# Attention and bilinear FFN in float32 on one core: softmax with keys on partitions and no maximum, head products issued in turn, FFN in blocks of 384 and 512 tokens

## The chip, the core and the metric

The kernel runs on one core of a Trainium2 chip. The metric is the device time of one execution in microseconds (us), median over runs. The engines named below are PE (TensorE, matmuls; PEld is its weight load), DVE (VectorE), ACT (ScalarE), POOL (GpSimd) and SP (SyncE), which here issues all DMAs. Each engine takes its instructions in program order.

## The reference, cut to what matters

```python
# q, k, v: (8, 12, 448, 64) float32; g_q, g_k: (64,); w_a, w_b: (768, 1536), w_out: (1536, 768), in float64
def rmsnorm(x, g):
    return x / np.sqrt(np.mean(x * x, axis=-1, keepdims=True) + 1e-06) * g
scores = np.matmul(rmsnorm(q, g_q), rmsnorm(k, g_k).transpose(0, 1, 3, 2)) / np.sqrt(64)
scores = scores - np.max(scores, axis=-1, keepdims=True)
attn = np.exp(scores)
attn = attn / (np.sum(attn, axis=-1, keepdims=True) + 1e-09)
x = np.matmul(attn, v).transpose(0, 2, 1, 3).reshape(8 * 448, 12 * 64)
out = ((x @ w_a) * (x @ w_b)) @ w_out
```

## The kernel before, in words

Everything is float32. There are 8 batches of 448 tokens and 12 heads of 64 features. Attention goes by pairs of heads (48 pairs, 6 in each batch), and inside a pair by quarters of 112 queries, so the main loop has 192 steps `i`, four to a pair. A pair's q and k are normalised (`normalize`: squares and a power on POOL, sums and products on DVE), transposed on PE and copied out of PSUM with the gains (`transpose_qk`).

A step `i` makes the scores of 112 queries against 448 keys for both heads (`scores`, L180: queries on partitions), their maximum (DVE, L183), the exponential with its sum (ACT, L184), and the division (POOL, L188). `transpose_e` turns the result round on PE (L198) and copies it out (L200 and L202), one step later. `values` multiplies it with v (L212) two steps later; all four products of the first head stand there ahead of those of the second.

The FFN of batch b - 1 fills PE during the attention of batch b. `ffn` is a generator that yields after each piece: 24 groups of six matmuls (tile `pf`, L229) and 16 half groups of six matmuls (tile `po`, L242). `some(share)` runs as many pieces as are due. It starts at step 2 of a batch and is drained at step 1 of the next, so that two steps of each batch have no pieces. Three PSUM banks (`ps_mm`) hold the FFN's results.

The weights come as float64 in 72 units of 128 x 384 numbers. `round_weights` makes float32 of one unit: six DVE instructions (L116 to L122), one on ACT (L123), two on POOL (L124, L125). Tiles `mag` and `low` have one buffer, so a unit's DVE work starts when POOL has read the `mag` of the unit before. Two units stand in each of the first 36 steps. The order of all instructions is the order in which the code is written (`manual_schedule`).

## Time and profile before

| | |
|---|---|
| median of 3 runs | 2462.69 us (2460.68 to 2463.14) |
| span of the profiled execution | 2462.0 us, which is 0.7 us under that median |
| PE busy | 2135.5 us, 87% of the span |
| POOL, DVE, ACT busy | 927.3, 863.8 and 507.3 us |
| granted TensorE clock, mean | 0.92 |

The profile covers one execution, from its first to its last instruction. Busy time is the time in which an engine executes; a float32 matmul appears in it as two records (two passes over the same columns), while a transpose is one. A granted clock of 1.00 is 2.4 GHz and 0.50 is 1.2 GHz.

### The profile page before, as it was taken

What the parts mean: (1) busy time and instruction counts of PE and PEld (TensorE: products, weight loads), DVE (VectorE), ACT (ScalarE), POOL (GpSimd) and SP (SyncE); (2) the same over time, 40 slices, a digit from 0 to 9 for tenths busy, and PEclk for the clock granted to TensorE, in tenths of its full rate; (3) what the DMA queues carried; (4) which work ended last, traced back from release to release, by engine and by line L of the source; (5) the groups of instructions that cost most, each with busy time, mean ns of one, the idle gap of its engine ahead of it and who ended that gap; (6) DMA issues with size and microseconds to landing.
All of it is one profiled execution on the core that took longest, in us unless ns stands there. A gap on an engine that the chain in (4) does not pass through costs nothing.

```text
span 2462.0 us, 24929 instructions
## 1 busy us (share of the span) xinstructions
PE 2135.5 (87%) x9600; PEld 1223.7 (50%) x9600; DVE 863.8 (35%) x1809; ACT 507.3 (21%) x1257; POOL 927.3 (38%) x679
## 2 busy tenths in 40 slices
PE   3444448889999998999899998999899989999999
PEld 1332224445555554555555564555455545555555
DVE  5666665663232232322322323223222323222000
ACT  1221122222222222222222122222222212222100
POOL 5656555553333343433423333333333343332000
PEclk9566558889999998999899998999999999999999
DMA  3222222110100010000100010001100010000000
GB/s 91 65 73 62 63 77 62 53 48 24 33 17 18 7 37 25 12 16 23 42 12 12 17 35 17 23 4 32 33 12 12 24 33 23 12 10 15 3 0 23
DMA packets 53558, 73.95 MB, mean 30 GB/s; under 512 B 4801, under 2 KB 44225, under 8 KB 53441
## 3 DMA queue, kind: packets, MB, share of 16 engines
q1 hardware_dynamic: 53440, 72.37, 10.3%
q8 instruction: 76, 1.25, 0.2%
q14 instruction: 42, 0.34, 0.0%
HBM read 61.34 MB, written 11.01 MB: 29 GB/s over the span
## 4 chain that ended last, share of the span: by engine, by line
PE 73%; DVE 14%; POOL 7%; issue 3%; ACT 3%; DMA 0%; SPq 0%; POOLq 0%; ACTq 0%; DVEq 0%
PE pf L229 32%; PE po L242 21%; PE o L212 8%; PE sc L180 6%; PE pt L198 5%; POOL ms L146 3%; ACT E L184 2%; DVE mag L118 2%; POOL sq L142 2%; POOL low L124 1%; POOL E L188 1%; DVE ms L143 1%; PE pt L161 1%; DVE qkn L149 1%; DVE nmax L183 1%
## 5 line engine op out<-in xcount | busy, mean ns | idle before, releaser
L188 POOL TENSOR_SCALAR E<-E,sums 112x448 f32<-112x448 f32 x384 | 538.0, 1413 | 1118.0 <-DVE sums L186 892.2
L242 PE MATMUL po<-w_out_sb,hT 128*112 128x384 f32 x1536 | 519.7, 490 | 0.0
L229 PE MATMUL pf<-xT,w_b_sb 128*128 128x448 f32 x1152 | 470.7, 560 | 13.1 <-ACT hT L232 13.1
L229 PE MATMUL pf<-xT,w_a_sb 128*128 128x448 f32 x1152 | 459.1, 548 | 6.6 <-ACT qkT L166 5.8
L198 PE MATMUL pt<-ident,E 112*112 112x112 f32 x1536 | 210.5, 280 | 272.8 <-ACT ET L202 173.4
L184 ACT ACTIVATE E<-sc,nmax 112x448 f32<-112x448 f32 x384 | 240.1, 630 | 853.3 <-DVE nmax L183 853.3
L242 PEld LDWEIGHTS po<-w_out_sb,hT 128*112 128x112 f32 x1536 | 262.6, 177 | 233.1 <-issue 42.3
L183 DVE TENSOR_REDUCE nmax<-sc 112x1 f32<-112x448 f32 x384 | 221.3, 618 | 405.8 <-PE sc L180 405.8
L198 PEld LDWEIGHTS pt<-ident,E 112*112 112x112 f32 x1536 | 171.0, 144 | 361.0 <-issue 326.0
L229 PEld LDWEIGHTS pf<-xT,w_b_sb 128*128 128x128 f32 x1152 | 219.4, 196 | 230.0 <-issue 216.5
L229 PEld LDWEIGHTS pf<-xT,w_a_sb 128*128 128x128 f32 x1152 | 213.9, 192 | 228.2 <-issue 219.2
L212 PEld LDWEIGHTS o<-ET,v 112*64 112x64 f32 x3072 | 261.7, 150 | 94.9 <-issue 90.8
L212 PE MATMUL o<-ET,v 112*64 112x112 f32 x3072 | 306.6, 287 | 0.0
L180 PE MATMUL sc<-qkT 64*112 64x448 f32 x768 | 215.2, 637 | 17.8 <-ACT E L184 17.1
L234 DVE TENSOR_TENSOR hT<-hT,pf 128x448 f32<-128x448 f32 x96 | 59.5, 619 | 303.1 <-PE pf L229 303.1
L146 POOL TENSOR_TENSOR ms<-ms,expo 112x16 f32<-112x16 f32 x48 | 140.7, 2931 | 48.4 <-DVE ms L145 48.4
L143 DVE TENSOR_REDUCE ms<-sq 112x8 f32<-112x512 f32 x96 | 65.8, 686 | 244.3 <-POOL sq L142 244.3
L200 DVE COPY ET<-pt 112x448 f32<-112x448 f32 x192 | 118.6, 618 | 64.9 <-PE pt L198 62.6
L202 ACT COPY ET<-pt 112x448 f32<-112x448 f32 x192 | 101.9, 531 | 154.1 <-PE pt L198 154.1
L124 POOL TENSOR_TENSOR low<-low,mag 128x384 f32<-128x384 f32 x72 | 71.7, 996 | 142.4 <-DVE mag L122 142.4
L142 POOL TENSOR_TENSOR sq<-qk 112x512 f32<-112x512 f32 x96 | 99.9, 1041 | 41.8 <-DVE ms L143 39.3
L149 DVE TENSOR_TENSOR qkn<-qk,ms 112x512 f32<-112x512 f32 x96 | 62.1, 689 | 146.1 <-POOL ms L146 146.1
(40 smaller groups left out, 827.1 us busy)
## 6 DMA issues: line engine op xcount, KB each, us to landing
qk<-in_q_dram SPq DMA_DIRECT2D x48, 224.0 KB, 3.3
qk<-in_k_dram SPq DMA_DIRECT2D x48, 224.0 KB, 3.5
v<-in_v_dram SPq DMA_DIRECT2D x48, 224.0 KB, 2.8
out_dram<-o_sb SPq DMA_DIRECT2D x64, 168.0 KB, 2.1
raw<-in_moe_w_a_dram SPq DMA_DIRECT2D x24, 384.0 KB, 3.2
raw<-in_moe_w_b_dram SPq DMA_DIRECT2D x24, 384.0 KB, 3.3
raw<-in_moe_w_out_dram SPq DMA_DIRECT2D x24, 384.0 KB, 3.2
gains<-in_g_q_dram SPq DMA_DIRECT2D x2, 0.2 KB, 3.2
```

The lines of the kernel that those rows point to most:

```text
L142: nc.gpsimd.tensor_tensor(sq, qk[:, s], qk[:, s], ALU.mult)
L146: nc.gpsimd.tensor_tensor(msf, msf, expo, ALU.pow)
L180: nc.tensor.matmul(sc, lhsT=qT[rows, j * SP:(j + 1) * SP], rhs=kT[rows, :], start=True, stop=True)
L183: nc.vector.reduce_max(nmax[:, e:e + 1], scs[e], axis=AX, negate=True)
L184: nc.scalar.activation(E[:, e], scs[e], AF.Exp, bias=nmax[:, e:e + 1], accum_out=sums[:, e:e + 1])
L188: nc.gpsimd.tensor_scalar_mul(E[:, e], E[:, e], sums[:, e:e + 1])
L198: nc.tensor.transpose(pt[:, cs], E[:, e, cs], ident[0:SP, 0:SP])
L200: nc.vector.tensor_copy(ETs[i][:, e], pt)
L202: nc.scalar.copy(ETs[i][:, e], pt)
L212: nc.tensor.matmul(os_[p][e * D:(e + 1) * D, j * SP:(j + 1) * SP], lhsT=vs[p][:, e, c * D:(c + 1) * D], rhs=ET[:, e, c * SP:(c + 1) * SP], ...
L229: nc.tensor.matmul(pf, lhsT=w_sb[:, c, m * P:(m + 1) * P], rhs=xT[:, c, :], start=(c == 0), stop=(c == KA - 1))
L242: nc.tensor.matmul(po, lhsT=hT[:, m, j * SP:(j + 1) * SP], rhs=w_out_sb[:, m, hs], start=(m == 0), stop=(m == KO - 1))
```

## The change

Scores are computed with the keys on partitions and the queries along the free axis. Their exponential then is already what the product with v needs, so the transposes of the exponential, their copies and the division on POOL are gone. No maximum is taken off; the gains' largest product decides by a branch behind the fast path whether a `general()` path, written like the reference, runs after it (it does where that product is over 72 / 8 = 9; with the seeded inputs it is 5.26). k is not normalised before its transposes; its inverse root mean square is the exponential's per-partition scale, and both gains go into q. The sums over keys come from three additions of the exponentials (one on DVE, two on POOL), a product with a tile of ones (`su`), a reciprocal and one multiplication of the attention's output (`divide`).

The main loop has 96 half steps `i`, two to a pair; h = i % 2. In `scores` and `values` the two heads' matmuls take turns, each 448 columns wide. The FFN has blocks of 384 and 512 tokens in turn, with two PSUM banks instead of three, and its pieces are spread by their cost over all 12 half steps of a batch, from the third half step on. A unit of weights takes four DVE, two ACT and two POOL instructions, from two load buffers instead of three. One unit stands in each of the first 12 half steps and six in each of the next ten.

```diff
+        nc.vector.tensor_scalar(small, grow[:, 1, 0:1], LIMIT * D ** -0.5, None, ALU.is_le)
...
+            nc.scalar.activation(magf, hi.bitcast(FP32), AF.Abs)
+            nc.vector.tensor_scalar(magf, magf, BELOW, ABOVE, ALU.max, ALU.min)
+            nc.vector.tensor_scalar(mag, mag, 3, 0x3FFFFFFF, ALU.logical_shift_left, ALU.bitwise_and)
+            nc.vector.scalar_tensor_tensor(wb, hi, 0xC0000000, mag, ALU.bitwise_and, ALU.bitwise_or)
+            nc.vector.tensor_scalar(mag, wb, 0xFF800000, None, ALU.bitwise_and)
+            nc.scalar.activation(low, lo, AF.Copy, scale=2.0 ** -52)
+            nc.gpsimd.tensor_tensor(low, low, magf, ALU.mult)
+            nc.gpsimd.tensor_tensor(w, w, low, ALU.add)
...
+        def scores(p, c):
+            qT, kT = qkTs[p][:, 0], qkTs[p][:, 1]
+            sc = ps_s.tile([SP, 2, 512], FP32, tag="sc", name="sc")
+            for e in range(2):
+                rows = slice(e * D, (e + 1) * D)
+                nc.tensor.matmul(sc[:, e, 0:S], lhsT=kT[rows, c * SP:(c + 1) * SP], rhs=qT[rows, :],
+                                 start=True, stop=True)
+            E = ETs[p, c] = wk.tile([SP, 2, S], FP32, tag="ET", name="ET", bufs=4)
+            for e in range(2):
+                nc.scalar.activation(E[:, e], sc[:, e, 0:S], AF.Exp, scale=rs[p][:, 1, 2 * c + e:2 * c + e + 1])
+
+        def add_up(p, c):
...
+                nc.vector.tensor_tensor(sums[p][0:SP], ETs[p, 0], ETs[p, 1], ALU.add)
+            elif c > 1:
+                nc.gpsimd.tensor_tensor(sums[p][0:SP], sums[p][0:SP], ETs[p, c], ALU.add)
+
+        def values(p, cs):
...
+            for c in cs:
+                E = ETs[p, c]
+                for e in range(2):
+                    nc.tensor.matmul(os_[p][e * D:(e + 1) * D, :], lhsT=vs[p][:, e, c * D:(c + 1) * D],
+                                     rhs=E[:, e], start=(c == 0), stop=(c == NJ - 1))
...
+        def divide(p):
...
+            for e in range(2):
+                nc.tensor.matmul(su[e * D:(e + 1) * D, :], lhsT=ones, rhs=sm[0:SP, e], start=True, stop=True)
+            rinv = sm[:, 0]
+            nc.vector.reciprocal(rinv, su)
...
+                nc.vector.tensor_tensor(x, x, rinv[:, frm:frm + size], ALU.mult)
...
+                if b > 0 and r == LAG:
+                    some(1e9)
+                    fill, due, done = ffn(b - 1), 0.0, 0.0
+                    total = sizes[b - 1] * (2 * KA + DM // P) * KO * 4 / 2400
+                share = total / (2 * HP) if fill is not None else 0.0
+                if h == 0:
+                    if p >= 1 and p <= NP:
+                        values(p - 1, (2, 3))
+                        put_out(p - 1)
+                    if p < NP:
+                        scores(p, 0)
+                        scores(p, 1)
+                        load(p + 1, "v")
+                        load(p + 2, "qk")
+                    some(share / 2)
+                    if p >= 1 and p <= NP:
+                        divide(p - 1)
+                    normalize(p + 1)
+                else:
+                    if p < NP:
+                        values(p, (0, 1))
+                        add_up(p, 1)
+                        scores(p, 2)
+                        add_up(p, 2)
+                        scores(p, 3)
+                        add_up(p, 3)
+                    some(share / 2)
+                    if p < NP:
+                        transpose_qk(p + 1)
+                upto = i + 1 if i < 12 else 12 + (i - 11) * 6
+                while todo < min(upto, len(units)):
+                    load_weights(loaded)
+                    loaded += 1
+                    round_weights(todo)
+                    todo += 1
+                some(share / 2)
...
+    fast()
+    fits = nc.values_load(small[0:1, 0:1], min_val=0, max_val=1)
+    with tc.If(fits == 0):
+        general()
```

PE in the FFN's first pieces, one step `i` of before (`pt<-ident,qkn` is the transposes of the next pair's q and k, every fourth step; `x6` and the like count matmuls):

```order
L229 MATMUL pf<-xT,w_a_sb 128x448 x6
L161 MATMUL pt<-ident,qkn 128x112 x8
L198 MATMUL pt<-ident,E 112x112 x8
L229 MATMUL pf<-xT,w_b_sb 128x448 x6
L212 MATMUL o<-ET,v 64x112 x8
L180 MATMUL sc<-qkT 112x448 x2
```

PE at the same place of the changed kernel, one pair (two half steps, h = 1 and then h = 0), in a block of 384 tokens:

```order
L227 MATMUL o<-ET,v_sb 64x448 x4
L207 MATMUL sc<-qkT 112x448 x4
L285 MATMUL pf<-xT,w_b_sb 128x384 x6
L193 MATMUL pt<-ident,k_sb 128x112 x4
L196 MATMUL pt<-ident,qn 128x112 x4
L285 MATMUL pf<-xT,w_a_sb 128x384 x6
L227 MATMUL o<-ET,v_sb 64x448 x4
L207 MATMUL sc<-qkT 112x448 x4
L285 MATMUL pf<-xT,w_b_sb 128x384 x6
L285 MATMUL pf<-xT,w_a_sb 128x384 x6
L270 MATMUL su<-sum,ones 64x448 x2
L285 MATMUL pf<-xT,w_b_sb 128x384 x6
```

A quarter's work of before (transposes, eight narrow products, two scores) became half a pair's work of four wide products and four scores, with FFN groups on both sides of the transposes or of `su`.

POOL in the first batch of before, one step `i` and the start of the next pair's normalisation:

```order
L124 TENSOR_TENSOR low<-low,mag 128x384
L125 TENSOR_TENSOR w_a_sb<-w_a_sb,low 128x384
L124 TENSOR_TENSOR low<-low,mag 128x384
L125 TENSOR_TENSOR w_b_sb<-w_b_sb,low 128x384
L188 TENSOR_SCALAR E<-E,sums 112x448 x2
L142 TENSOR_TENSOR sq<-qk 112x512 x2
L146 TENSOR_TENSOR ms<-ms,expo 112x16
```

POOL of the changed kernel from half step 11 (the last with one unit) into half step 12 (the first with six):

```order
L219 TENSOR_TENSOR sum<-sum,ET 112x896 x2
L144 TENSOR_TENSOR low<-low,mag 128x384
L145 TENSOR_TENSOR w_b_sb<-w_b_sb,low 128x384
L172 TENSOR_TENSOR sq<-q_sb 112x512
L172 TENSOR_TENSOR sq<-k_sb 112x512
L176 TENSOR_TENSOR ms<-ms,expo 112x16
L144 TENSOR_TENSOR low<-low,mag 128x384
L145 TENSOR_TENSOR w_a_sb<-w_a_sb,low 128x384
L144 TENSOR_TENSOR low<-low,mag 128x384
L145 TENSOR_TENSOR w_b_sb<-w_b_sb,low 128x384
```

The divisions L188 are gone, two wide additions stand once in each pair, and behind the normalisation the units follow one another instead of two in each step.

## Rows read from the trace of the kernel before

**Rows 1.** The page: span, granted clock in 40 slices, chain that ended last by line.

```profile
span 2462.0 us, 24929 instructions
...
PEclk9566558889999998999899998999999999999999
...
PE pf L229 32%; PE po L242 21%; PE o L212 8%; PE sc L180 6%; PE pt L198 5%; POOL ms L146 3%; ACT E L184 2%; DVE mag L118 2%; POOL sq L142 2%; POOL low L124 1%; POOL E L188 1%; DVE ms L143 1%; PE pt L161 1%; DVE qkn L149 1%; DVE nmax L183 1%
```

**Rows 2.** Stages: window, its length, busy us of PE, PEld, DVE, ACT, POOL.

```profile
16.00:400.00 384.00, 173.81 (x802) 112.17 (x801) 252.67 (x503) 81.31 (x205) 224.14 (x183) 0.65 0.25 68
...
530.00:2288.00 1758.00, 1680.61 (x7888) 963.21 (x7887) 519.19 (x1127) 386.78 (x965) 631.30 (x432) 0.97 0.07 20
```

**Rows 3.** Timeline of PE in a filled step: start us, us, what.

```profile
1303.14 4.69 PE L229 MATMUL pf<-xT,w_a_sb 128*128 128x448 f32 x12
1307.76 1.42 PE L212 MATMUL o<-ET,v 112*64 112x112 f32 x16
1309.11 1.01 PE L180 MATMUL sc<-qkT 64*112 64x448 f32 x4
1310.05 4.78 PE L229 MATMUL pf<-xT,w_b_sb 128*128 128x448 f32 x12
1314.66 0.93 PE L198 MATMUL pt<-ident,E 112*112 112x112 f32 x8
1315.43 4.69 PE L229 MATMUL pf<-xT,w_a_sb 128*128 128x448 f32 x12
```

**Rows 4.** Timeline of PE in the last batch's FFN (first, ninth group; end).

```profile
2296.95 4.67 PE L229 MATMUL pf<-xT,w_a_sb 128*128 128x448 f32 x12
...
2333.03 4.67 PE L229 MATMUL pf<-xT,w_a_sb 128*128 128x448 f32 x12
...
2396.16 62.08 PE L242 MATMUL po<-w_out_sb,hT 128*112 128x384 f32 x192
```

**Rows 5.** Timeline of normalisations: the second pair's, then the powers of two later pairs.

```profile
22.07 1.04 POOL L142 TENSOR_TENSOR sq<-qk 112x512 f32<-112x512 f32 x1
...
28.93 1.29 DVE L149 TENSOR_TENSOR qkn<-qk,ms 112x512 f32<-112x512 f32 x2 [3.05 <-POOL ms L146]
...
80.72 2.93 POOL L146 TENSOR_TENSOR ms<-ms,expo 112x16 f32<-112x16 f32 x1 [1.01 <-DVE ms L145]
...
135.83 2.93 POOL L146 TENSOR_TENSOR ms<-ms,expo 112x16 f32<-112x16 f32 x1 [1.01 <-DVE ms L145]
```

**Rows 6.** Timeline of one unit of weights, from the POOL product of the unit before.

```profile
154.01 0.99 POOL L124 TENSOR_TENSOR low<-low,mag 128x384 f32<-128x384 f32 x1 [0.78 <-DVE mag L122]
...
155.08 1.16 POOL L125 TENSOR_TENSOR w_a_sb<-w_a_sb,low 128x384 f32<-128x384 f32 x1
155.43 1.03 DVE L118 TENSOR_SCALAR mag<-mag 128x384 f32<-128x384 f32 x1
156.28 0.55 ACT L123 ACTIVATE low<-raw 128x384 f32<-128x384 uint32 x1 [6.10 <-POOL w_a_sb L125]
...
157.49 0.56 DVE L121 SCALAR_TENSOR_TENSOR w_b_sb<-raw,w_b_sb 128x384 uint32<-128x384 uint32 x1
...
158.08 0.36 DVE L122 TENSOR_SCALAR mag<-w_b_sb 128x384 uint32<-128x384 uint32 x1
...
158.58 0.99 POOL L124 TENSOR_TENSOR low<-low,mag 128x384 f32<-128x384 f32 x1 [2.34 <-DVE mag L122]
```

**Rows 7.** Lines by form: busy us, mean ns of one, idle before.

```profile
L234 DVE TENSOR_TENSOR hT<-hT,pf 128x448 f32<-128x448 f32 x96 | 59.5, 619 | 303.1 <-PE pf L229 303.1
...
L186 DVE RECIPROCAL sums<-sums 112x2 f32<-112x2 f32 x192 | 31.8, 166 | 6.9 <-DVE sums L185 0.4
...
L84 DVE TENSOR_SCALAR gains<-gains 128x1 f32<-128x1 f32 x1 | 0.2, 154 | 5.8 <-DMA gains<-in_g_q_dram 5.8
```

**Rows 8.** Timeline of PE: scores of the first step with FFN pieces, and nine later.

```profile
372.16 1.63 PE L180 MATMUL sc<-qkT 64*112 64x448 f32 x4
...
526.61 1.01 PE L180 MATMUL sc<-qkT 64*112 64x448 f32 x4
```

**Rows 9.** DMA issues of a unit: count, KB each, median us to landing.

```profile
raw<-in_moe_w_a_dram SPq DMA_DIRECT2D x24, 384.0 KB, 3.2
```

More of the change, by code (lines that the diff above doesn't have):

```diff
@@ L254 @@
-    PIECES = 2 * KO + 4 * NJ
-    LAG = 2
-    fill, due, done = None, 0.0, 0
-    def some(share):
-        nonlocal due, done
-        due += share
-        while fill is not None and done < due:
-            next(fill, None)
-            done += 1
-    with tc.manual_schedule():
-        load(0)
-        setup()
-        load(1)
-        for n in range(2):
-            load_weights(n)
-        normalize(0)
-        transpose_qk(0)
-        for i in range(NS + LAG):
-            p, j = divmod(i, NJ)
-            b, r = divmod(i, HP * NJ)
-            if b > 0 and r == LAG:
-                fill, due, done = ffn(b - 1), 0.0, 0
-            share = PIECES / (HP * NJ - LAG) / 2
-            if i < NS:
-                scores(i)
-                if j == 0 and p + 1 < NP:
-                    normalize(p + 1)
-                if j == 1 and p + 2 < NP:
-                    load(p + 2)
-                for n in range(2 * i, 2 * i + 2):
-                    load_weights(n + 2)
-                    round_weights(n)
-            some(share)
-            if j == 2 and p + 1 < NP:
-                transpose_qk(p + 1)
-            if 1 <= i <= NS:
-                transpose_e(i - 1)
-            some(share)
-            if i >= LAG:
-                values(i - LAG)
-            if fill is not None and r == LAG - 1:
-                for _ in fill:
-                    pass
-                fill = None
-        for _ in ffn(B - 1):
-            pass
@@ new lines, in fast_body @@
+        ETs, sums, os_, xTs, tails = {}, {}, {}, {}, {}
+        def scores(p, c):
[8 more added lines that the diff above has]
+                nc.scalar.activation(E[:, e], sc[:, e, 0:S], AF.Exp, scale=rs[p][:, 1, 2 * c + e:2 * c + e + 1])
@@ new lines, in fast_body, with places, open_block @@
+        ends = []
+        for b in range(B):
+            ends.append((b + 1) * S // P * P)
+        sizes = [e - s for s, e in zip([0] + ends, ends)]
+        OVER = S - sizes[0]
+        def places(b):
+            start = ends[b - 1] if b else 0
+            at = b * S - start
+            n = min(S, ends[b] - b * S)
+            got = [(xTs, b, at, 0, n)]
+            if n < S:
+                got.append((tails, b + 1, 0, n, S - n))
+            return got
+        def open_block(b):
+            xTs[b] = wk.tile([P, KA, 512], FP32, tag="xT", name="xT", bufs=2)
+            if b in tails:
+                n = b * S - ends[b - 1]
+                nc.gpsimd.tensor_copy(xTs[b][:, :, 0:n], tails.pop(b))
+            if ends[b] < (b + 1) * S:
+                tails[b + 1] = wk.tile([P, KA, (b + 1) * S - ends[b]], FP32, tag="tail", name="tail")
@@ new lines, in store @@
+        def store(b, t, hs, o_sb):
+            g, end = ends[b] - sizes[b] + t * P, ends[b] - sizes[b] + (t + 1) * P
+            at = 0
+            while g < end:
+                bb, r = divmod(g, S)
+                j, p0 = divmod(r, SP)
+                n = min(end - g, SP - p0)
+                rows = out[bb * S:(bb + 1) * S].rearrange("(p j) d -> j p d", j=NJ)
+                nc.sync.dma_start(rows[j][p0:p0 + n, hs], o_sb[at:at + n])
+                g, at = g + n, at + n
+        fill, due, done = None, 0.0, 0.0
@@ new lines, in some @@
+        def some(share):
+            nonlocal fill, due, done
+            due += share
+            while fill is not None and done < due:
+                took = next(fill, None)
+                if took is None:
+                    fill = None
+                else:
+                    done += took
+        NH = 2 * NP
+        LAG = 3
+        with tc.manual_schedule():
+            load(0, "qkv")
+            setup(wk)
+            load(1, "qk")
+            for n in range(2):
+                load_weights(n)
+            normalize(0)
+            transpose_qk(0)
+            todo, loaded = 0, 2
+            for i in range(NH + LAG):
+                p, h = divmod(i, 2)
+                b, r = divmod(i, 2 * HP)
+                if b > 0 and r == LAG:
[3 more added lines that the diff above has]
+                share = total / (2 * HP) if fill is not None else 0.0
+                if h == 0:
+                    if p >= 1 and p <= NP:
[10 more added lines that the diff above has]
+                    normalize(p + 1)
+                else:
+                    if p < NP:
[15 more added lines that the diff above has]
+                some(share / 2)
+            some(1e9)
+            fill, due, done = ffn(B - 1), 0.0, 0.0
+            some(1e9)
```

358 lines of the change are left out of this document (207 added, 151 removed).

## Prediction

> **What bounds the kernel now.** I read the page first: the clock slices, then the chain that ended last [rows 1]. The reader is to see two regimes. In the first six or seven slices PE is granted about half its clock; behind that it is nearly always near full, and the chain is mostly PE's FFN lines (32% and 21%). The windows put numbers to it [rows 2]: from 16 to 400 us PE is busy 174 of 384 us at a mean clock of 0.65, and no engine is full (DVE 253, POOL 224), so a chain through several engines bounds it; from 530 to 2288 us PE is busy 1681 of 1758 us.
>
> In the filled stretch PE sets the pace. A step's groups follow each other without a gap [rows 3]: six float32 matmuls of 448 columns take 4.61 to 4.62 us from start to start, the transposes 0.77, the products with v 1.35, the two scores 0.94. Behind one another, the groups of the last batch take (2333.03 - 2296.95) / 8 = 4.51 us, or 0.376 for one pass over 448 columns [rows 4], so a change of product costs about 0.10. The last batch's `po` takes 62.08 us, and 2462.0 - 2458.2 = 3.8 us follow it.
>
> The first stretch goes by pairs: the power of the normalisation comes every 135.83 - 80.72 = 55.1 us [rows 5]. A pair holds eight units of weights. From one unit's POOL product to the next 158.58 - 154.01 = 4.57 us pass [rows 6], 36.6 us for the eight; the rest is the normalisation and attention's own waits, in line with them on DVE and POOL.
>
> **The filled stretch.** What is removed there (maximum, division, copies) lies beside PE and gains nothing by itself; it gains in the first batch. What counts is PE's work.
>
> FFN: the 192 `pf` groups keep their total of columns: 192 x 4.51 = 866 us. `po` falls from 768 to 672 matmuls of 384 columns: 8 x 62.08 x 7/8 = 434.6 us. Sum 1300.5, where before it was 1362.5.
>
> Attention: the two scores take 0.94 us, though their four passes of 0.376 would take 1.50 one by one [rows 3]: the heads run side by side, as 2 x 0.376 and 0.19 around them. In `values` of before 16 passes of 112 columns take 1.35 us, where eight transposes of 112 columns take 0.77: two passes' worth is hidden, at the seam of the heads. I take it that turns hide half of all, as in the scores. A half step then has four passes for v and four for scores (2 x 1.69 = 3.38), the way back into FFN twice (0.20), and either `su` (2 x 0.376 + 0.19 = 0.94) or the transposes (0.77), 0.86 in the mean: 4.45 us.
>
> I see no stall behind PE here. ACT's eight exponentials of a pair, by L123's 0.55 for 384 columns, are some 5 us of about 36 [rows 6]. The longest chain is `su`, reciprocal, normalisation, transposes: about 8 us, while FFN pieces and products keep PE busy for about 15 us between `su` and the transposes (the rows of the order of PE). The two steps of a batch without pieces are gone, and with them the clock's dips.
>
> **The first batch and the weights.** A new unit is: exponent part on ACT (0.55 like L123), L139, which waits for POOL's L145 of the unit before and ends 0.22 us behind it, as L118 ends at 156.46 and L125 at 156.24, that is 1.45 us from the release; then 0.36, 0.56 and 0.36 with gaps of 0.04, 0.15 to POOL, and 0.99 [rows 6]: 4.0 us, against 4.57. `mag` and `low` still have one buffer, so units can't overlap more.
>
> Normalisation: 28.93 - 22.07 = 6.86 us from the first square to the product, and one product instead of two, 0.65 [rows 5]: 7.5. With the first unit's DVE work free of POOL (1.76), 0.15 and 0.99 it takes 10.4 us to that unit's L144. In h = 1, L145 (1.23) and two additions on POOL come first. An addition of 896 is not in the trace; by the square (1.04 for 512) it is 1.8 us, by L124 (0.99 for 384) 2.3; I take 1.9, nearer to the first. L139 and L140 end behind them at 5.25, and L144 at 7.4 us.
> - Start, to the second pair's squares: 8.66 + 2.93, 12 us; the start is as before.
> - Six pairs with one unit in each half: 10.4 + 7.4 + 1.2 = 19.0 us, 114 us. PE's own work (2 x 3.38 + 1.71, 8.5 us, or 17 at half clock) lies beside it.
> - Five pairs with six units in each half: 5 x (19.0 + 10 x 4.0) = 295 us.
> - FFN pieces inside this stretch, from half step 15 to 21: PE runs at most two groups ahead, whose banks are emptied only behind the units, and `su` or the transposes wait behind those groups. Before, nine such steps take 526.61 - 372.16 = 154.4 us [rows 8], 30.4 more than at 55.1 / 4 each, for 16.4 pieces: 1.86 us a piece. Seven twelfths of the first block's FFN (139.3 us x 7/12 = 81.3) are 21 groups: 39 us.
>
> Behind half step 21 PE has left 1300.5 - 81.3 = 1219 us of FFN and 74 half steps x 4.45 = 329 us.
>
> **Costs not shown.** The reciprocal of 448 sums: as a plain operation on as many it is 0.62 us (L234). The reciprocal of two numbers takes 166 ns, 12 more than the shortest DVE row, at most 6 ns for each, so 2.85 us at most [rows 7]. I take 0.7, as two numbers cost no more than a plain operation; then it lies beside POOL's additions. At 2.85 it adds about 2.2 us in nine places, 20 us. The branch: an engine must load a value and jump. I take 3.3 us, one DMA round trip by [rows 9], between nothing (beside the last store) and two of them. The k loads in runs of 256 bytes are fetched a pair ahead, 19 us, and cost nothing unless they take that long. Two load buffers: a unit's load starts some 1.5 us before its L144 and takes about 0.4 + 3.2 us; its data is due 4.0 us behind that L144, so 1.9 us are spare.
>
> On the reciprocal, the Trainium skill ("VectorE: DVE Perf Modes", the section on the fixed hardware budget) says that it is an iterative divide with a repeat count of 8, not a single pass. At eight cycles a number that would be an estimated 3.9 us, and the sum some 29 us longer than mine; no row here has a wide reciprocal, and the row of two speaks for less.
>
> **Sum.** 12 + 114 + 295 + 39 + 1219 + 329 + 3.8 + 3.3 = 2015 us as a span; the median of the runs is 0.7 above the profiled span, so 2016 us, 18% under 2462.69.
>
> **Rivals.**
> - *The heads' products with v and ones do not run side by side.* For it: L212's 16 passes hide only two. Price: per pair 8 + 2 passes of 0.376, 3.76 us, for 37 pairs 139 us: 2155 us. Chance 0.10.
> - *A unit of the burst takes 6 us, not 4.0*, because two load buffers behind SP's queue of q, k and v leave it waiting for data. For it: 3.2 us of landing against 1.9 spare; against it: before, the loads never end a wait in the chain [rows 1]. 60 x 2 = 120 us: 2136 us. Chance 0.10.
> - *The chain from `su` to the transposes does not hide in the filled stretch*: 2 us in each half step, 148 us: 2164 us. Against it: 8 us of chain, 15 of cover. Chance 0.06.
> - *The burst costs less*, the FFN pieces in it running beside the units and the normalisation beginning ahead of them: 39 us of the pieces and 5 us in each of 5 pairs: 1952 us. Chance 0.09.
> - *Slower: two FFN banks instead of three leave a gap behind each group*, so that PE is granted half its clock as in the first stretch [rows 2]. Of the 1548 us behind the burst 446 would have to be worked at 1.2 GHz, taking twice as long, to reach 2462; if all were, it would be 3564 us. Against it: a group is emptied in 0.62 us (L234) while the next takes 3.9 to 5.1 [rows 4, 7]. Chance 0.03.
> - *The branch runs the general path too*: at least another FFN of 1300 us, over 3300 us. The inputs' product of 5.26 against 9 excludes it but for an error. Chance 0.01.
>
> **Numbers.** My forecast, 2016 us, has 0.61. Its own range is 1960 to 2080: the reciprocal's 20 us, 11 us of the additions, 30 us either way for the pieces in the burst and the start. For 8 in 10 I go down to the cheaper burst and up to the 6 us unit, 1945 to 2140, which leaves out 0.20. A measurement of this kernel tells about 0.2% from no change. Faster by more than that 0.95, slower 0.04, the same 0.01, since only the clock and the branch end there.
>
> **What would show it.** Right: powers of the normalisation about 19 us apart in the first batch and about 59 to 70 in the burst, ending near 460 us; POOL's L144 every 4.0 us inside; no PE gap behind it; `o` of four matmuls in about 1.7 us. Wrong: passes of `o` in line, 3 us; L138 waiting for a DMA; a granted clock under 1.00 behind the burst; a reciprocal over 3 us.

## The result and the profile after

The changed kernel takes 2006.61 us (median of 4 runs, 2006.35 to 2008.87), 0.8152 of the time before (95% interval 0.8141 to 0.8164): 18.5% faster. The forecast was 2016 us, so the direction, the size and the range held. That the sum behind it, 2015 us as a span, came within 10.5 us of the 2004.6 measured is in part luck: four of its terms were off by 3 to 12 us, in both directions.

The page of the changed kernel, its span, granted clock in 40 slices, the chain that ended last by line, and two groups of instructions (busy us, mean ns of one, idle before):

```profile
span 2004.6 us, 15250 instructions
...
PEclk9885777779999999999999999999999999999999
...
PE pf L285 42%; PE po L298 22%; PE sc L207 6%; PE o L227 6%; POOL low L144 3%; PE su L270 2%; DVE mag L139 2%; POOL ms L176 2%; DVE sum L272 1%; POOL sum L219 1%; DVE mag L140 1%; ACT mag L138 1%; DVE mag L142 1%; PE pt L196 1%; PE pt L193 1%
...
L219 POOL TENSOR_TENSOR sum<-sum,ET 112x896 f32<-112x896 f32 x96 | 200.0, 2084 | 130.4 <-ACT ET L211 79.2
L272 DVE RECIPROCAL sum<-su 128x448 f32<-128x448 f32 x48 | 141.9, 2957 | 270.8 <-PE su L270 270.8
```

Windows of its burst (half steps 12 to 21, with six units of weights each) and of its filled stretch behind it, where FFN pieces fill PE (columns as in [rows 2], then the granted clock):

```profile
138.00:460.00 322.00, 155.28 (x492) 77.17 (x491) 164.65 (x293) 94.86 (x181) 170.04 (x148) 0.73 0.31 85
460.00:2000.00 1540.00, 1538.70 (x4981) 746.54 (x4979) 341.79 (x424) 260.10 (x495) 332.18 (x184) 1.00 0.08 23
```

The two regimes of [rows 2] are still there, and the second is now full: behind 460 us PE is busy 1538.7 of 1540 us at full clock, where before it was 1681 of 1758 at 0.97. (Its last row ends at 1998.7, so the 1.3 us missing are the end of the window and not a gap.) In the burst (138 to 460) PE is busy less than half the time, and DVE and POOL only a little over half each: once more a chain through several engines.

POOL's timeline in the changed kernel, first the start, then the powers of the normalisation at the borders of the stages (start us, us, what, idle before it and its releaser; they answer to [rows 5]):

```profile
8.64 1.04 POOL L172 TENSOR_TENSOR sq<-q_sb 112x512 f32<-112x512 f32 x1 [7.20 <-DVE small L93]
...
15.41 1.04 POOL L172 TENSOR_TENSOR sq<-q_sb 112x512 f32<-112x512 f32 x1
...
22.07 2.90 POOL L176 TENSOR_TENSOR ms<-ms,expo 112x16 f32<-112x16 f32 x1 [1.01 <-DVE ms L175]
...
142.98 2.91 POOL L176 TENSOR_TENSOR ms<-ms,expo 112x16 f32<-112x16 f32 x1 [1.01 <-DVE ms L175]
...
201.56 2.91 POOL L176 TENSOR_TENSOR ms<-ms,expo 112x16 f32<-112x16 f32 x1 [1.01 <-DVE ms L175]
...
465.19 2.91 POOL L176 TENSOR_TENSOR ms<-ms,expo 112x16 f32<-112x16 f32 x1 [1.01 <-DVE ms L175]
...
497.45 2.91 POOL L176 TENSOR_TENSOR ms<-ms,expo 112x16 f32<-112x16 f32 x1 [1.01 <-DVE ms L175]
...
897.75 2.91 POOL L176 TENSOR_TENSOR ms<-ms,expo 112x16 f32<-112x16 f32 x1 [1.01 <-DVE ms L175]
```

Read as pairs: six with few weights take (142.98 - 22.07) / 6 = 20.15 us; the burst's first, still without FFN pieces, 58.58; the other four (465.19 - 201.56) / 4 = 65.9; the first filled pair 32.26. Before, a pair of the first batch took 55.1.

One unit of weights inside the burst, from POOL's product L144 of the unit before to its own (all engines; answers to [rows 6]):

```profile
214.60 0.99 POOL L144 TENSOR_TENSOR low<-low,mag 128x384 f32<-128x384 f32 x1 [1.74 <-DVE mag L142]
215.63 0.55 ACT L138 ACTIVATE mag<-raw 128x384 f32<-128x384 f32 x1 [2.18 <-POOL low L144]
215.67 1.00 POOL L145 TENSOR_TENSOR w_a_sb<-w_a_sb,low 128x384 f32<-128x384 f32 x1
216.21 0.68 DVE L139 TENSOR_SCALAR mag<-mag 128x384 f32<-128x384 f32 x1 [1.75 <-ACT mag L138]
...
216.92 0.36 DVE L140 TENSOR_SCALAR mag<-mag 128x384 uint32<-128x384 uint32 x1
217.31 0.56 DVE L141 SCALAR_TENSOR_TENSOR w_b_sb<-raw,mag 128x384 uint32<-128x384 uint32 x1
217.91 0.36 DVE L142 TENSOR_SCALAR mag<-w_b_sb 128x384 uint32<-128x384 uint32 x1
...
218.41 0.99 POOL L144 TENSOR_TENSOR low<-low,mag 128x384 f32<-128x384 f32 x1 [1.74 <-DVE mag L142]
```

Every step waits for the one above it but L145: 3.81 us, through the one buffer of `mag`.

PE's timeline, two places: `o` and the scores in the filled stretch, and an FFN group in the burst with what it waited for:

```profile
252.67 6.42 PE L285 MATMUL pf<-xT,w_a_sb 128*128 128x384 f32 x12 [12.66 <-ACT hT L288]
259.02 0.97 PE L270 MATMUL su<-sum,ones 112*64 112x448 f32 x4
...
612.01 1.72 PE L227 MATMUL o<-ET,v_sb 112*64 112x448 f32 x8
613.66 1.76 PE L207 MATMUL sc<-qkT 64*112 64x448 f32 x8
615.35 1.13 PE L285 MATMUL pf<-xT,w_b_sb 128*128 128x512 f32 x2
```

Eight passes of `o` take 1.65 us and eight of the scores 1.69, as predicted. In the burst PE stands 12.66 us for a copy of `hT` on ACT, and `su` comes behind the group that waited.

### The profile page after: what moved, and what is told of

Its sections match the earlier page's. It is cut to its first block, busy times and chain, and to the rows that moved or that the text cites. A ratio compares the mean times of both kernels' runs of the same rounds, so it can differ in the third digit from the quotient of the medians.

```text
span 2004.6 us, 15250 instructions
## 1 busy us (share of the span) xinstructions
PE 1769.9 (88%) x5760; PEld 851.6 (42%) x5760; DVE 594.9 (30%) x824; ACT 404.9 (20%) x773; POOL 590.6 (29%) x396
## 2 busy tenths in 40 slices
DMA packets 87318, 73.43 MB, mean 37 GB/s; under 512 B 49348, under 2 KB 78020, under 8 KB 87236
## 4 chain that ended last, share of the span: by engine, by line
PE 80%; DVE 9%; POOL 7%; ACT 2%; issue 1%; SPq 0%; DMA 0%; POOLq 0%; DVEq 0%; ACTq 0%
PE pf L285 42%; PE po L298 22%; PE sc L207 6%; PE o L227 6%; POOL low L144 3%; PE su L270 2%; DVE mag L139 2%; POOL ms L176 2%; DVE sum L272 1%; POOL sum L219 1%; DVE mag L140 1%; ACT mag L138 1%; DVE mag L142 1%; PE pt L196 1%; PE pt L193 1%
## 5 line engine op out<-in xcount | busy, mean ns | idle before, releaser
L285 PE MATMUL pf<-xT,w_b_sb 128*128 128x512 f32 (+1 forms) x1152 | 460.4, 550 | 58.5 <-DVE hT L290 39.6
L285 PE MATMUL pf<-xT,w_a_sb 128*128 128x512 f32 (+1 forms) x1152 | 461.8, 551 | 43.1 <-ACT hT L288 43.1
L298 PE MATMUL po<-w_out_sb,hT 128*128 128x384 f32 x1344 | 446.7, 489 | 0.0
L298 PEld LDWEIGHTS po<-w_out_sb,hT 128*128 128x128 f32 x1344 | 251.2, 190 | 191.9 <-issue 28.4
L211 ACT ACTIVATE ET<-sc,ms 112x448 f32<-112x448 f32 x384 | 212.4, 637 | 243.8 <-PE sc L207 240.9
L219 POOL TENSOR_TENSOR sum<-sum,ET 112x896 f32<-112x896 f32 x96 | 200.0, 2084 | 130.4 <-ACT ET L211 79.2
L272 DVE RECIPROCAL sum<-su 128x448 f32<-128x448 f32 x48 | 141.9, 2957 | 270.8 <-PE su L270 270.8
L290 DVE TENSOR_TENSOR hT<-hT,pf 128x384 f32<-128x384 f32 (+1 forms) x96 | 59.4, 619 | 513.4 <-PE pf L285 513.0
L227 PE MATMUL o<-ET,v_sb 112*64 112x448 f32 x768 | 180.8, 594 | 19.2 <-ACT ET L211 19.2
L144 POOL TENSOR_TENSOR low<-low,mag 128x384 f32<-128x384 f32 x72 | 76.9, 1069 | 132.9 <-DVE mag L142 110.9
L207 PEld LDWEIGHTS sc<-qkT 64*112 64x112 f32 x768 | 62.6, 177 | 114.8 <-issue 103.1
L138 ACT ACTIVATE mag<-raw 128x384 f32<-128x384 f32 x72 | 39.8, 553 | 192.4 <-POOL low L144 192.4
```

The lines of the kernel that those rows point to most:

```text
L138: nc.scalar.activation(magf, hi.bitcast(FP32), AF.Abs)
L144: nc.gpsimd.tensor_tensor(low, low, magf, ALU.mult)
L207: nc.tensor.matmul(sc[:, e, 0:S], lhsT=kT[rows, c * SP:(c + 1) * SP], rhs=qT[rows, :], start=True, stop=True)
L211: nc.scalar.activation(E[:, e], sc[:, e, 0:S], AF.Exp, scale=rs[p][:, 1, 2 * c + e:2 * c + e + 1])
L219: nc.gpsimd.tensor_tensor(sums[p][0:SP], sums[p][0:SP], ETs[p, c], ALU.add)
L227: nc.tensor.matmul(os_[p][e * D:(e + 1) * D, :], lhsT=vs[p][:, e, c * D:(c + 1) * D], rhs=E[:, e], start=(c == 0), stop=(c == NJ - 1))
```

## Experiments

Differences are against the changed kernel's 2006.61 us, where nothing else is named.

### e1: the heads' products with v apart

```diff
-                        values(p - 1, (2, 3))
-                        put_out(p - 1)
+                        values(p - 1, (2, 3), (0,))
                     ...
                         scores(p, 0)
+                        values(p - 1, (2, 3), (1,))
+                        put_out(p - 1)
                         scores(p, 1)
```

(and in h = 1 likewise around `scores(p, 2)`; the third argument of `values` names the heads)

> The products of v of the second head stand behind those of the first, with the scores of one quarter between them, so that no pass of one head can run beside one of the other. In the changed kernel the eight passes take 1.65 us (612.01 to 613.66), where eight of 0.376 in line would take 3.01. Theory, that they run side by side: 1.36 us more and two more changes of product of 0.1 to 0.2 us in each half step, in the 74 half steps in which PE sets the pace 1.56 to 1.76 us each, 115 to 130 us: 2120 to 2140 us. Rival, that eight passes take 1.65 us whichever head they are of, and the gain came from elsewhere: only the changes of product, 15 to 30 us: 2020 to 2037 us.

Measured: 2141.50 us (2141.11 to 2141.75), 134.9 more, just above the theory's range and far above the rival's. PE's timeline in the filled stretch:

```profile
601.04 1.72 PE L227 MATMUL o<-ET,v_sb 112*64 112x448 f32 x4
602.69 1.01 PE L207 MATMUL sc<-qkT 64*112 64x448 f32 x4
603.63 1.72 PE L227 MATMUL o<-ET,v_sb 112*64 112x448 f32 x4
605.28 1.01 PE L207 MATMUL sc<-qkT 64*112 64x448 f32 x4
606.22 5.42 PE L285 MATMUL pf<-xT,w_b_sb 128*128 128x512 f32 x12
```

Four passes of one head alone take 1.65 us, as long as eight of both in turns. From the first `o` to the FFN group 5.18 us pass, in the changed kernel 3.34: 1.84 x 74 = 136 us. The heads run side by side. The 1.84 us are four passes in line, 4 x 0.376 = 1.50, and two more changes of product, 0.15 and 0.19. The expectation had the changes, but only 1.36 for the passes: the 1.65 that it took off 3.01 holds a change itself.

### e2: FFN blocks of 448 tokens

```diff
-            ends.append((b + 1) * S // P * P)
+            ends.append((b + 1) * S)
...
-            for t in range(N // P):
+            for t in range(N // SP):
```

> The FFN goes back to blocks of 448 tokens, with four po tiles of 112 tokens for each batch, as before; all else stays. Theory, that a po matmul costs its 384 columns whatever rows it fills: 768 matmuls instead of 672, 62 us more: 2065 to 2072 us, and filled pairs of equal length, about 36 us, instead of 32.3 and 39.9 in turn. Rival, that blocks of unlike size cost something at their borders (tails copied, groups of 512 with longer copies): less than 62, 2035 to 2060 us.

Measured: 2058.94 us (2058.26 to 2061.03), 52.3 more: less than the theory gave, and by the number alone inside the rival's range. Powers at the burst's start and end and twelve pairs (two batches) on:

```profile
142.74 2.91 POOL L176 TENSOR_TENSOR ms<-ms,expo 112x16 f32<-112x16 f32 x1 [1.01 <-DVE ms L175]
...
475.23 2.91 POOL L176 TENSOR_TENSOR ms<-ms,expo 112x16 f32<-112x16 f32 x1 [1.01 <-DVE ms L175]
...
923.02 2.91 POOL L176 TENSOR_TENSOR ms<-ms,expo 112x16 f32<-112x16 f32 x1 [1.01 <-DVE ms L175]
```

Two filled batches take 447.79 us against 897.75 - 465.19 = 432.56: 7.6 us a batch, 61 for eight, so the theory's price of a `po` matmul (62 us for all) is right, and the borders of blocks of unlike size cost nothing that shows. The total is smaller because of where the added work stands: the first block is 31 us longer, 7/12 of that, 18 us, falls into the burst, and the burst grows by 10 only (332.5 against 322.2). 61 - 18 + 10 = 53. One detail of the theory failed: the filled pairs are not equal, but take 35.4 to 40.5 us.

### e3: no reciprocal

```diff
-            nc.vector.reciprocal(rinv, su)
+            nc.vector.tensor_copy(rinv, su)
```

> The reciprocal of the sums is replaced by a copy of them, so the attention's output is multiplied by the sums and not divided by them. A row of the changed kernel has 2957 ns for a reciprocal and 532 to 637 ns for copies or exponentials as wide, so 2.3 us less for each of 48. Theory (the prediction's): it counts only in the burst and the first batch where it stands between units or ahead of the normalisation, nine places, 20 us at most, or 6 x 0.7 + 4 x 2.3 = 13 us where DVE waits for nothing else: 1985 to 1995 us. Rival one, hidden everywhere: 2004 to 2009 us. Rival two, the chain from su to the transposes isn't hidden in the filled stretch: 2.3 us in each of 48 pairs, 110 us: 1897 us.

Measured: 1997.89 us (1997.45 to 1998.15), 8.7 less, between the ranges of the theory and of rival one. The power that ends the burst stands here at 453.83, 11.4 us earlier than in the changed kernel (465.19); 2.8 of them come from the first six pairs. The filled pairs take the same 32.3 and 39.9 us in both:

```profile
140.23 2.91 POOL L176 TENSOR_TENSOR ms<-ms,expo 112x16 f32<-112x16 f32 x1 [1.01 <-DVE ms L175]
...
453.83 2.91 POOL L176 TENSOR_TENSOR ms<-ms,expo 112x16 f32<-112x16 f32 x1 [1.01 <-DVE ms L175]
```

The chain from `su` to the transposes is hidden in the filled stretch, as the prediction had it; rival two would have needed 1897. In front the wide reciprocal costs 9 to 11 us, about half of the 20 that the prediction gave for it.

### e4: the head of a unit freed from mag

```diff
-            nc.scalar.activation(magf, hi.bitcast(FP32), AF.Abs)
-            nc.vector.tensor_scalar(magf, magf, BELOW, ABOVE, ALU.max, ALU.min)
-            nc.vector.tensor_scalar(mag, mag, 3, 0x3FFFFFFF, ALU.logical_shift_left, ALU.bitwise_and)
-            nc.vector.scalar_tensor_tensor(wb, hi, 0xC0000000, mag, ALU.bitwise_and, ALU.bitwise_or)
+            nc.scalar.activation(w, hi.bitcast(FP32), AF.Abs)
+            nc.vector.tensor_scalar(w, w, BELOW, ABOVE, ALU.max, ALU.min)
+            nc.vector.tensor_scalar(wb, wb, 3, 0x3FFFFFFF, ALU.logical_shift_left, ALU.bitwise_and)
+            nc.vector.scalar_tensor_tensor(wb, hi, 0xC0000000, wb, ALU.bitwise_and, ALU.bitwise_or)
```

> The first three steps of a unit of weights (L138 to L141) work in place in the weight's own tile instead of mag, so that they no longer wait for POOL's product L144 of the unit before; mag is written by L142 alone. Theory (the prediction's, that the wait for the single mag sets a unit's 3.81 us): the unit falls to the next loop, POOL L145 1.00, ACT L143 0.55, POOL L144 0.99 and about 0.15 between them, 2.7 us: 60 units x 1.1 = 66 us less in the burst, and up to 20 less in the first batch: 1920 to 1942 us. Rival one, two load buffers: a load starts when L143 has read the buffer and lands 3.5 us later, and L138 to L142 (2.3 us) follow it before the L144 two units on, 6.3 us for two units, so 3.1 to 3.3 us each: 1965 to 1975 us, and L138 waiting for a DMA. Rival two, the burst is bound by other things (PE, the half steps' borders): within 1% of the changed kernel, 1990 to 2010 us.

Measured: 1988.39 us (1987.24 to 1990.53), 18.2 less: a gain, but a fraction of the 66 us expected; by the number it is nearest to rival two (0.9% under the changed kernel). DVE and POOL in the burst:

```profile
207.81 0.99 POOL L144 TENSOR_TENSOR low<-low,mag 128x384 f32<-128x384 f32 x1 [1.02 <-DVE mag L142]
208.02 1.00 DVE L139 TENSOR_SCALAR w_a_sb<-w_a_sb 128x384 f32<-128x384 f32 x1 [0.36 <-ACT w_a_sb L138]
208.88 0.99 POOL L145 TENSOR_TENSOR w_b_sb<-w_b_sb,low 128x384 f32<-128x384 f32 x1
209.05 1.04 DVE L140 TENSOR_SCALAR w_a_sb<-w_a_sb 128x384 uint32<-128x384 uint32 x1
...
221.07 1.72 POOL L144 TENSOR_TENSOR low<-low,mag 128x384 f32<-128x384 f32 x1 [1.02 <-DVE mag L142]
```

The wait for `mag` is gone, yet the unit still takes (221.07 - 207.81) / 4 = 3.32 us. L139 and L140, 0.36 us alone, take 1.0 beside a POOL product and end 0.2 behind its end. So the chain was real, but close beneath it lies something like the sum of the two engines' work (1.64 on DVE and 1.99 on POOL are 3.63, less what slips between); e5 tests that. An instruction that reads PSUM is not held: the changed kernel's reciprocal keeps its 2.96 us with a POOL product inside it.

```profile
136.50 2.96 DVE L272 RECIPROCAL sum<-su 128x448 f32<-128x448 f32 x1 [0.33 <-PE su L270]
...
137.38 1.00 POOL L145 TENSOR_TENSOR w_b_sb<-w_b_sb,low 128x384 f32<-128x384 f32 x1
```

The burst's first pair falls by 4.9 us, ten times 0.49; the four with FFN pieces by 3.5 each, so part of the gain is lost there. In the first batch nothing is gained: its six pairs take 20.6 us each, as they do in e7 and e9 (20.5), which leave that stretch as it was.

### e5: the unit's products on DVE

```diff
-            nc.gpsimd.tensor_tensor(low, low, magf, ALU.mult)
-            nc.gpsimd.tensor_tensor(w, w, low, ALU.add)
+            nc.vector.tensor_tensor(low, low, magf, ALU.mult)
+            nc.vector.tensor_tensor(w, w, low, ALU.add)
```

(on top of e4)

> As e4_free_head, and a unit's two products and sums L144 and L145 move from POOL to DVE. In e4 a unit took 3.3 us and not the 2.7 of its loop: DVE's L139 to L141, 0.36, 0.36 and 0.56 us alone, showed 1.0, 1.05 and 1.24 beside L144 or L145, and ended some 0.2 to 0.4 behind them. Theory, that DVE stands still while POOL works on a tile of weights, so that a unit costs the sum of both (1.64 + 1.99 less what slips between): with everything on DVE it is 0.36 + 0.36 + 0.56 + 0.36 + 2 x 0.56 and 6 gaps of 0.04, 3.0 us: 60 x 0.3 = 18 us under e4's 1988, 1965 to 1975 us. Rival, that the two engines do work side by side and the long rows are waits for POOL's results: DVE then has 1.1 us more to do in each unit, which takes up to 4.4: 2030 to 2060 us.

Measured: 1974.79 us (1972.71 to 1975.27), 13.6 under e4 and at the theory's upper end. Giving DVE more work made the kernel faster, which the rival can't explain. A unit of the burst takes 2.91 us, and the burst 282.3 where it took 303.2 in e4. In the first six pairs, with two units each, the same edit costs 1.0 us a pair (21.6 for 20.6).

### e6: nothing on POOL but the power

```diff
-                nc.gpsimd.tensor_tensor(sums[p][0:SP], sums[p][0:SP], ETs[p, c], ALU.add)
+                nc.vector.tensor_tensor(sums[p][0:SP], sums[p][0:SP], ETs[p, c], ALU.add)
...
-                nc.gpsimd.tensor_tensor(sq, flat, flat, ALU.mult)
+                nc.scalar.activation(sq, flat, AF.Square)
```

(on top of e5)

> As e5_products_on_dve, with the two additions of the exponentials L219 moved from POOL to DVE (the addition L217, as wide, takes 1.08 us there against 2.08 on POOL) and the squares L172 from POOL to ACT; POOL keeps the power. Theory, that in the burst DVE is what counts once POOL no longer holds it up: a pair has 12 units x 3.0 and, on DVE beside them, reciprocal and product 3.6, sums and powers 5, qn 0.7 and three additions and a copy 4, 49 us and with FFN pieces some 53, against 58.6 and 66: 65 to 75 us under the changed kernel's 2006.6, 1930 to 1945 us. Rival, that the additions and squares were in nobody's way: no more than e5, 1965 to 1975 us.

Measured: 1970.90 us (1969.59 to 1971.48), only 3.9 under e5: the theory falls, and the rival's range holds it. Its timeline, the unit and then a border of half steps:

```profile
209.91 0.56 DVE L144 TENSOR_TENSOR low<-low,mag 128x384 f32<-128x384 f32 x1
...
212.82 0.56 DVE L144 TENSOR_TENSOR low<-low,mag 128x384 f32<-128x384 f32 x1
...
242.70 6.06 PE L285 MATMUL pf<-xT,w_a_sb 128*128 128x384 f32 x12 [6.86 <-ACT hT L288]
...
248.70 0.97 PE L270 MATMUL su<-sum,ones 112*64 112x448 f32 x4
...
249.72 2.96 DVE L272 RECIPROCAL sum<-su 128x448 f32<-128x448 f32 x1 [4.64 <-PE su L270]
```

A unit is 2.91 us, as in e5, and the burst's pair without FFN pieces takes 48.7 us, as reckoned (49). But at the border DVE waits 4.64 us for `su`, which stands behind an FFN group, which had waited 6.86 us for ACT's copy of `hT`, which stands in ACT's order behind the six units. The theory had left out that wait. DVE has it in each of the four pairs with pieces, 4.6 to 5.2 us, nearly as in e5 (4.7 to 5.5), and they take 57.0 us where 53 were reckoned. The start loses 3.6 us besides: the second pair's power stands at 25.70, in e5 at 22.06.

### e7: the first block's FFN later

```diff
-                if b > 0 and r == LAG:
+                if (b > 1 and r == LAG) or i == 21:
...
-                share = total / (2 * HP) if fill is not None else 0.0
+                share = total / (2 * HP if b > 2 or (b == 2 and r >= LAG) else 6) if fill is not None else 0.0
```

> The changed kernel, but the first block's FFN begins six half steps later (half step 21 instead of 15) and has its pieces in half the number of steps, so that nearly none of them stands in the burst of weights. Theory (the prediction's 39 us for 21 pieces inside the burst, or 11 us in each pair): the burst's five pairs fall from 322 us to 5 x 58.6 = 293, and PE does the 70 to 81 us of pieces behind it: 40 to 55 us longer, 2047 to 2062 us. Rival one, that the pieces lie in time in which PE has nothing else to do and cost the burst nothing: its pairs stay near 65 us, and the time grows by 70 to 81: 2077 to 2088 us. Rival two, that the pieces cost as much as they do elsewhere: no change, 2000 to 2015 us.

Measured: 2062.80 us (2061.32 to 2063.54), 56.2 more, 0.8 us above the theory's range and far from both rivals.

```profile
203.88 2.91 POOL L176 TENSOR_TENSOR ms<-ms,expo 112x16 f32<-112x16 f32 x1 [1.01 <-DVE ms L175]
...
378.18 2.91 POOL L176 TENSOR_TENSOR ms<-ms,expo 112x16 f32<-112x16 f32 x1 [1.01 <-DVE ms L175]
```

Three pairs of the burst without pieces take 58.1 us each, against 65.9 with them. So the 21 groups cost the burst 465.19 - 201.56 - 4 x 58.1 = 31 us, 1.5 each; done elsewhere they cost an estimated 81 (139.3 x 7/12).

### e8: no branch

```diff
-    fits = nc.values_load(small[0:1, 0:1], min_val=0, max_val=1)
-    with tc.If(fits == 0):
-        general()
```

> The changed kernel without the branch and the general path behind it (the gains' product is not looked at). The last copy of the FFN's result is followed by 5.3 us to the end of the span, where before 3.8 us followed the last matmul, and the median lies 2.0 above the span against 0.7. Theory, that these are the branch's: 2 to 5 us less, 2001.5 to 2004.5 us. Rival, that the branch lies beside the last store and costs nothing: 2005.5 to 2007.5 us.

Measured: 2005.89 us (2005.31 to 2006.78), ratio 0.8150 (0.8137 to 0.8164) against 0.8152: no difference that can be told. The rival holds; the branch costs at most about 1 us.

### e9: FFN pieces between the units

```diff
+                left = min(upto, len(units)) - todo
                 while todo < min(upto, len(units)):
                     ...
                     todo += 1
-                some(share / 2)
+                    some(share / 2 / left)
+                if left <= 0:
+                    some(share / 2)
```

(on the changed kernel; nothing of e4 to e6)

> The changed kernel, with the second half of a half step's FFN pieces spread between the six units of weights, a sixth behind each unit, instead of all behind the last. In e7 the burst's pairs took 58.1 us without pieces, with them 65 to 67 us in the changed kernel. Theory, that a piece costs there what its copies out of PSUM wait: they stand on ACT and DVE behind six units (a row has 18.90 us of PE behind the copy of hT), and the product su or the transposes stand behind the pieces on PE; with pieces between units only the copies themselves are left, two to three DVE products of 0.56 and as much on ACT in a pair, so that the pairs fall to 60 to 61 us: 3.5 x 5 = 17 us less, 1985 to 1993 us. Rival, that the pieces cost by what they take from ACT and DVE wherever they stand, or by PE's half clock: 2002 to 2010 us.

Measured: 1982.09 us (1980.57 to 1982.57), 24.5 less, more than the theory gave.

```profile
145.28 2.91 POOL L176 TENSOR_TENSOR ms<-ms,expo 112x16 f32<-112x16 f32 x1 [1.01 <-DVE ms L175]
...
437.79 2.91 POOL L176 TENSOR_TENSOR ms<-ms,expo 112x16 f32<-112x16 f32 x1 [1.01 <-DVE ms L175]
```

All five pairs take 58.5 us, as long as a pair without pieces: not even their copies out of PSUM show. The same pieces, the same work; only where their copies stand in ACT's and DVE's order differs. That order was their whole price in the burst. The burst is 29.7 us shorter than in the changed kernel (292.5 against 322.2). It begins 2.3 us later, as in e7, though neither edit touches what stands ahead of it, and the first filled pair takes 2.8 us more.

### e10, e11, e12: the start rebuilt

e10 joins e6 and e9 and adds three edits:

```diff
+                    norm_a(p + 1)          # squares, sums, power: ahead of values, scores and divide
                     ...
-                    normalize(p + 1)
+                    norm_b(p + 1)          # the product qn
...
+            for c in range(NJ):            # sum_up, pairs 0 to 11, in place of add_up
+                for e in range(2):
+                    nc.tensor.matmul(su[e * D:(e + 1) * D, :], lhsT=ones, rhs=ETs[p, c][:, e],
+                                     start=(c == 0), stop=(c == NJ - 1))
...
-                upto = i + 1 if i < 12 else 12 + (i - 11) * 6
+                upto = min(3 * (i + 1) if i < 12 else 36 + 4 * (i - 11), len(units))
```

e11 is e10 with the old line for `upto`; e12 is e10 without `sum_up`.

> As e6_no_pool, and: units of weights three in each of the first 12 half steps and four in each of the next nine, instead of one and then six; FFN pieces between the units as in e9; squares, sums and power of the next pair ahead of the division, so that the power (2.9 us on POOL) lies beside the reciprocal (2.96 us on DVE); in the first 12 pairs, where PE has time, the sums over keys come from eight products with ones and not from three additions and two products. Theory, that in e6 DVE's work and its waits at the half steps' borders set the first 21 half steps (72 units x 2.91 = 210 us; border work 9.6 + 4 us a pair and some 5 us behind su): borders fall from about 11 us a half step to 5 to 7, so the units are ready after 10 + 210 + 21 x 6 = 346 us, with six half steps' FFN pieces done (70 us); behind it PE has 1300 - 70 + 75 x 4.45 = 1564 us and 8 us of end: 1900 to 1930 us. Rival, that the borders are bound by PE's and ACT's waits in their own order, which the edits don't shorten: no more than the squares' part, 1955 to 1971 us.

> As e10_rebuilt_start, with the units of weights again one in each of the first 12 half steps and six in each of the next ten. Theory, that DVE's work sets this stretch wherever the units stand: in e10 a pair took 25.7 us with six units, 8.2 of it not the units' 2.91 each; so six pairs with two units of 14 us and five with twelve of 43 to 45, in all 299 to 309 us, where e10 took 333.5 - 20.3 = 313 for the same eleven pairs: 1880 to 1895 us, no loss. Rival, that the spread was a good part of e10's gain, since PE is left waiting in the burst and has its FFN pieces before it: 1910 us or more.

> As e10_rebuilt_start, with the sums over keys of the first 12 pairs again from three additions on DVE (1.09 us each) and two products instead of eight products. Theory, that DVE sets the first eleven pairs: 3.3 us in each, 25 to 36 us more: 1918 to 1930 us. Rival, that the additions stand where DVE waits for the exponentials anyway: 1890 to 1900 us.

Measured: e10 1893.27 us (1892.41 to 1894.09), e11 1867.04 (1867.01 to 1867.31), e12 1908.03 (1907.01 to 1908.17). Powers of the second, eighth and thirteenth pair of e10, and of e11:

```profile
20.56 2.91 POOL L177 TENSOR_TENSOR ms<-ms,expo 112x16 f32<-112x16 f32 x1 [5.34 <-DVE ms L176]
...
174.44 2.90 POOL L177 TENSOR_TENSOR ms<-ms,expo 112x16 f32<-112x16 f32 x1 [22.80 <-ACT ET L217]
...
333.75 2.90 POOL L177 TENSOR_TENSOR ms<-ms,expo 112x16 f32<-112x16 f32 x1 [23.33 <-DVE ms L176]
```

```profile
20.56 2.90 POOL L177 TENSOR_TENSOR ms<-ms,expo 112x16 f32<-112x16 f32 x1 [5.34 <-DVE ms L176]
...
97.93 2.90 POOL L177 TENSOR_TENSOR ms<-ms,expo 112x16 f32<-112x16 f32 x1 [9.96 <-ACT ET L217]
...
316.89 2.90 POOL L177 TENSOR_TENSOR ms<-ms,expo 112x16 f32<-112x16 f32 x1 [40.66 <-ACT ET L217]
```

e10 went 7 us below its theory's range; the last unit was ready at about 324 us, where 346 were expected. Of its edits only two were undone by themselves, the place of the units (e11) and the sums on PE (e12); what the earlier normalisation gives alone stays open. e11's theory, that the units cost the same wherever they stand, held for the first six pairs (25.6 us with six units, 12.9 with two: 3.2 a unit), and it named the right sign; the gain, 26.2 us, is over the 0 to 13 it gave. Five pairs with twelve units took 43.8 each. Of the gain 16.9 us lie ahead of the thirteenth pair's power (316.89 against 333.75), the other 9 behind it; a possible reason for these, that in e10 units remained for half steps in which PE already set the pace, so that PE waited early and DVE late, was not tried by itself. In e12 the additions cost 14.8 us, half of what the theory gave and far over the rival's nothing: in the first six pairs 2.2 us each, where their time on DVE is 3.3, so a third of it lies where DVE would have waited.

e11 is the best version, 0.7585 of the time before (0.7570 to 0.7600), or 0.7585 / 0.8152 = 0.930 of the changed kernel's.

## Why the prediction was right, step by step

- **The filled stretch** (1219 + 329 us). Right to the term. A pair in a block of 384 tokens was to take 139.3 / 6 + 2 x 4.45 = 32.1 us and took 32.26; twelve pairs over both kinds of block were to take 431.9 and took 432.56. e1 shows the half of it that was in doubt, e2 the `po` term. From the burst's end to the end of the program it is 9 us less than reckoned, of which about 1 is the end's. The rest is a matter of the border: when `su` of half step 22 runs (457.77), PE has done that half step's products with v and scores (3.34 us) and 23 FFN groups, two more than the 21 counted into the burst (2 x 3.87). That is an estimated 11 us which the sum puts behind the burst, where 8 are missing.
- **The heads side by side** (1.69 + 1.69 us a half step, rival at 2155): 1.65 + 1.69. e1 sets the products with v apart, as that rival has them, and takes 2141.
- **The chain from `su` to the transposes hidden** (rival at 2164): e3 shows it.
- **Two banks** (the slower rival): behind 460 us PE is busy without a gap to its last row, at full clock.
- **Two load buffers** (rival at 2136): a unit was 3.81 us, not 6; in the unit's rows L138 is released by POOL's product, not by a load. (With units of 2.91 us, in e5 and e6, L138 does wait about 1 us for its load; DVE's rows follow each other without a gap all the same.)
- **A unit of 4.0 us through the one buffer of `mag`**: 3.81, and the steps are those of the sum. But e4 shows that the buffer is not all that holds it: without that wait it is 3.32, since DVE stands still while POOL works (e5). Of this the trace before had shown the edge (L118 at 1.03 us beside L125 in [rows 6]; the same step takes 0.35 in e6, where POOL is idle), and the sum had taken it as a wait in the chain, which gave the right number and would have given a wrong one for e4. The Trainium skill ("SBUF — State Buffer", the section on its two separate sides) has it as a lock: the two engines share a pair of ports, and a POOL instruction and a DVE instruction in one of its two-port modes exclude each other for the whole of an instruction; so do a DVE instruction with two SBUF inputs and a POOL instruction that reads SBUF. The traces agree: 0.36 us became 1.04 beside L145, and the reciprocal, which reads PSUM, kept its 2.96 us.
- **Six pairs at 19.0 us**: 20.15, mis-sized by 7 us in all. The additions on POOL took 2.08 us each where 1.9 was taken, and the reciprocal has 0.46 us of each pair (e3); the rest, some 0.3 a pair, was not traced.
- **The reciprocal** (0.7 us, at most 2.85): 2957 ns, over the bound. The step that failed is the inference from two numbers to 448: 12 ns over the shortest row don't bound what one more number costs, since that row, an operation on one number, has 154 of the 166 ns already; it took 6.6 ns for each of 448. The Trainium skill ("VectorE: DVE Perf Modes", the section on the fixed hardware budget) had spoken against it, with an iterative divide; the trace agrees that it isn't one plain pass (619 ns for as many), and is under the estimate of 3.9 us made from it. e3 prices the whole at 9 us: of 11 x 2.3 = 25 us in the pairs in front, the larger part is hidden.
- **FFN pieces inside the burst**: 39 us taken, 30 to 31 measured (e7, e9). The reason given, banks emptied only behind the units, is shown by e9. The rival of a cheaper burst (1952) did not come true by itself: the pieces cost those 30 us here, and nothing in e9.
- **Pairs of the burst without their pieces**: 5 x (19.0 + 10 x 4.0) = 295 taken, 5 x 58.5 = 293 measured in e9.
- **Start, 12 us, "as before"**: 15.41. `grow` lies in the buffer of `sq`, and POOL's first square waits 7.20 us for DVE's L93, the last reader of it, which waits for the gains: a wait that the order of the instructions doesn't show, but the tag in the code does.
- **Branch and end, 3.3 + 3.8 us**: 5.9 behind PE's last row, and e8 gives at most about 1 us of it to the branch. The 3.3 were taken from a DMA round trip; that the branch lies beside the last store is likely, but no row shows it. At 2006 us the general path can't have run.

Summed: + 3.4 (start) + 6.9 (six pairs) - 11.8 (burst with pieces, 322.2 for 334) - 9.0 (filled and end) = - 10.5 us, the span's 2004.6 for 2015.

## What to carry to other kernels

Where a fill-in engine's results are emptied by engines that have a burst of other work, the price of a piece is where its copy stands in their order: put pieces between the parts of the burst, not behind them. A chain through one buffer and two engines that exclude each other give the same row; before buying a second buffer, read whether the short instruction gets longer only beside the other engine, and if so move its work, not its buffer. A row of a few numbers doesn't price the same operation on hundreds.

## What the runs showed of the hardware

- DVE and POOL, both on SBUF tiles, take turns: 0.36 us becomes 1.04 beside a POOL product of 0.99, and the burst's units went from 3.32 us (e4) to 2.91 (e5, e6) by giving POOL's two products to DVE, where each takes 0.56.
- A reciprocal of 128 x 448 numbers out of PSUM takes 2957 ns, 6.6 ns for each along the free axis, against 1.4 for a plain product (619 ns).
- In the burst, an FFN group that had waited 12.66 us took 6.35 us (252.67 to 259.02), where 12 such passes take 4.0 at full clock (1715.08 to 1719.05); the granted clock over the burst is 0.73.
- Of 87318 DMA packets 49348 are shorter than 512 bytes. By its size k makes an estimated 43008 of them (11.0 MB in runs of 256 bytes); no wait for its loads lies in the chain.
